# Window attention and a maxout layer in chunks of 256 tokens: h of the later chunks two chunks at a time, and written-out slots

## The chip, the cores and the metric

The kernel runs on one core of a Trainium2 chip. Its time is the device time of one launch in microseconds (us), given as the median of several runs, with the lowest and the highest beside it. One further execution is recorded by the hardware profiler; its span runs from the first to the last instruction.

## The reference

Attention over a sliding window of 128 positions, plus the first four positions of each sequence as "sinks", and behind it a layer that takes the largest of three products:

```python
# q, k, v: [4, 8, 768, 64], float32
scores = scale * np.matmul(q, k.transpose(0, 1, 3, 2))
...
in_window = (rel >= 0) & (rel < int(window))
keep = is_sink | in_window
scores = np.where(keep, scores, -1000000000.0)
...
a = np.exp(scores)
a = a / (np.sum(a, axis=-1, keepdims=True) + 1e-09)
attn_out = np.matmul(a, v)
...
# x: [3072, 512]; w1, w2, w3: [512, 768]; w_out: [768, 512]
h = np.maximum(np.maximum(x @ w1, x @ w2), x @ w3)
return (h @ w_out).astype(np.float32)
```

There are 4 batches of 768 tokens, 8 heads of 64, and 3072 tokens in the second part.

## The kernel before

The tokens are cut into 12 chunks of 256, three for each batch (`CPB`); each partition holds two neighbouring tokens, and heads go in four pairs. A chunk passes these steps, each a function that is called with the chunk's number:

- `load` (L90) brings q, k and v as float32 on SyncE's (SP's) DMA queue, 512 KB each. The raw tiles have two buffers, so the load of chunk c waits until chunk c-2 has been cast. A gate (`pool_gate`, `after`) is a tiny instruction on POOL that holds a load back until POOL, or a weight, has come that far.
- `cast_qk` (L102) and `cast_v` (L108) write bf16 copies, on POOL, ACT or VectorE (DVE), whichever the call names.
- `turn` and `turn2` transpose q and k on TensorE for the first four chunks; from chunk 4 on `turn_dma` (L157, L162) does it with DMA transposes on SP's queue, two issues for k and one for q. The transposed tiles (`kT`, `qT`) and `vb` are rings of four.
- `score` (L278): six matmuls for each head pair into two PSUM banks; `expo` (L290) takes the exponentials on ACT and frees the banks; `mask` (L296) zeroes on VectorE what lies outside the window. `premask` adds a mask on TensorE instead, for some pairs at the start.
- `sink_k`, `sink_score` (L304, L310), `sink_v` (L320): the same for the four sink tokens.
- `av` (L354, and L336 for the sinks): probabilities times v, with a column of ones for the sum; VectorE takes the reciprocal (L359) and writes x (`x_sb`, L362).
- `xpose` (L375) transposes x on TensorE for chunks 0 to 3, `xpose_dma` (L381) by DMA on SP's queue for the others.
- `ffn_h(ci, fp, wi)` (L394): eight matmuls of 256 columns, two blocks of 128 hidden units for one of the three weights, into one PSUM bank. The first weight's bank is copied by ACT (L401), the other two are folded in by VectorE with a maximum (L405). A chunk has nine such groups.
- `ffn_y` (L415): six matmuls of 512 columns for each half of a chunk, then a copy by ACT or VectorE (L417), and `store` (L431) on SP's queue. The last chunk's second half goes in two parts (`ffn_y_part`, L425; `store_half`).

PSUM has eight banks; `bank` hands them out in the order in which `give` returned them while the program was written, so that a step waits for the release of the bank that it was given. `warm` runs matmuls on zeros at the start. TensorE is PE in the views.

The order is set by hand: each engine executes its instructions in the order of the calls, and SP's queue issues its DMAs in that order too. Chunks 0 to 3 are listed call by call. Behind them a loop runs over slots: slot i scores chunk i+1, computes h of chunk i and y of chunk i-1, and loads, casts and transposes chunk i+3, with a fixed order for all slots but the first and the last two.

Of the kernel before, what the change touches and what calls it, by code (L numbers as in the profile page):

```python
# [9 lines left out]
F32 = mybir.dt.float32  # L10
# [6 lines left out]
def kernel(  # L17
# [31 lines left out]
    with tc.manual_schedule():  # L49
# [316 lines left out]
        xTs = {}  # L366

# [39 lines left out]

        ys = {}

        def ffn_y(ci, t, eng=None):  # L410
# [3 lines left out]
            for fb in range(FB):  # L414
                nc.tensor.matmul(yp, lhsT=hs[ci][:, fb, t * 128:(t + 1) * 128], rhs=wo[:, fb],  # L415
# [4 lines left out]
        def ffn_y_part(ci, t, c0, c1, eng):  # L420
# [3 lines left out]
            for fb in range(FB):  # L424
                nc.tensor.matmul(yp, lhsT=hs[ci][:, fb, t * 128:(t + 1) * 128],  # L425
# [33 lines left out]
        load(0, 'q', gate=pool_gate)  # L459
        masks()  # L460
        cast_qk(0, 'q', 1, nc.vector)
        warm(4)
        premask(0, (2,))
        premask(0, (0,))
        warm(9)
        cast_qk(0, 'k', 0, nc.scalar)
        turn(0, 'k', 0, nc.vector)
        load(0, 'v')
        cast_qk(0, 'q', 0, nc.scalar)
        turn(0, 'q', 1, nc.vector)  # L470
        sink_init()
        warm(1)
        cast_qk(0, 'k', 1, nc.gpsimd)
        cast_v(0, 1, 0, nc.vector)
        turn(0, 'k', 1, nc.scalar)
        load(1, 'k')
        turn(0, 'q', 0, nc.scalar)
        cast_v(0, 0, 1, nc.vector)
        score(0, (2,))
        masks_late()  # L480
        premask(0, (1,))
        load_w(0, 512, 768)
        load_w(0, 0, 512)
        cast_v(0, 0, 0, nc.vector)
        load(1, 'q')
        score(0, (0,))
        sink_k(0)
        expo(0, 2)
        load_w(1, 512, 768)
        cast_qk(1, 'k', 0, nc.vector)  # L490
        expo(0, 0)
        premask(0, (3,))
        cast_v(0, 1, 1, nc.vector)
        cast_qk(1, 'q', 0, nc.gpsimd)
        score(0, (1,))
        premask(1, (1,))
        turn2(1, 'k', 0, nc.vector)
        cast_qk(1, 'k', 1, nc.scalar)
        score(0, (3,))
        expo(0, 1)  # L500
        cast_qk(1, 'q', 1, nc.gpsimd)
        load(1, 'v')
        turn2(1, 'k', 1, nc.scalar)
        expo(0, 3)
        av_open(0)
        av(0, 0)
        av(0, 1)
        sink_v(0)
        turn2(1, 'q', 0, nc.vector)
        load_w(1, 0, 512)  # L510
# [385 lines left out]
```

## Time and profile before

| | |
|---|---|
| median of 3 runs | 179.18 us (179.01 to 179.55) |
| the profiled execution | 179.04 us, of it 177.3 us span |
| mean granted TensorE clock | 0.996 of full speed |
| L394, h matmuls of 256 columns | 864, 100.7 us busy |
| L415, y matmuls of 512 columns | 138, 32.4 us busy |
| L290, exponentials on ACT | 96, 46.6 us busy |
| L405, maxima on VectorE | 74, 49.2 us busy |
| data moved | 34.90 MB, 197 GB/s mean |

A duration of a matmul in the groups is longer than its share of the time, because matmuls overlap; where the text needs what one adds, it takes a stretch of the chain of waits and divides by the count. The share of busy time is a mean over the whole program: what a wait costs is read in the stretch in which it stands.

### The profile page before, as it was taken

The page shows a single profiled execution, that of the slowest core. Times are in us where ns is not written, and L with a number is a line of the kernel's source. Part 1 is how long each engine was busy: PE and PEld are TensorE (multiplying, and loading weights), DVE is VectorE, ACT ScalarE, POOL GpSimd, SP SyncE. Part 2 cuts the span into 40 slices and gives each one's busy share as a digit, 9 for nine tenths or more (in the row PEclk, how much of TensorE's full clock was granted, in tenths as well). Part 3 has the DMA queues.
Part 4 walks back from the last instruction along what each step waited for, and adds up shares of the span by engine and source line. Part 5 has one row for each costly group of instructions (what it writes and reads, how often), then busy time and mean ns, then how long its engine had stood idle before and what let it go on. Part 6 is the DMA issues. An engine that isn't in the chain of part 4 may idle for free.

```text
span 177.3 us, 4632 instructions
## 1 busy us (share of the span) xinstructions
PE 170.1 (96%) x1872; PEld 127.1 (72%) x1872; DVE 126.5 (71%) x267; ACT 85.8 (48%) x171; POOL 67.1 (38%) x123
## 2 busy tenths in 40 slices
PE   6899999999998999999999999999999999999991
PEld 2446889856895597697696696796795895796870
DVE  3389738699698578796884984975885875966451
ACT  3498732577924822913724814814616617320210
POOL 6884344146580274544724624417427000000000
PEclk9999999999999999999999999999999999999998
DMA  5999999995999969999999999999999519305203
GB/s 141 290 287 203 224 248 259 216 265 148 290 140 236 94 142 299 129 245 173 251 269 189 210 301 160 213 303 153 198 293 198 150 34 379 125 11 170 120 0 118
DMA packets 69573, 34.90 MB, mean 197 GB/s; under 512 B 26544, under 2 KB 68016, under 8 KB 69552
## 3 DMA queue, kind: packets, MB, share of 16 engines
q1 hardware_dynamic: 64912, 31.33, 81.3%
q0 software_dynamic: 4496, 3.15, 11.6%
q8 instruction: 14, 0.23, 0.5%
q10 hardware_dynamic: 144, 0.13, 0.2%
q14 instruction: 7, 0.06, 0.1%
HBM read 25.17 MB, written 6.29 MB: 177 GB/s over the span
## 4 chain that ended last, share of the span: by engine, by line
PE 87%; DMA 4%; DVE 3%; SPq 2%; POOL 1%; ACT 1%; issue 0%; POOLq 0%
PE h_ps L394 52%; PE y_ps L415 18%; PE o L354 6%; PE st L278 6%; DMA q_raw<-in_q_dram 4%; SPq L90 2%; DVE h_sb L405 1%; PE o L336 1%; PE sk L304 1%; PE pt L118 1%; PE y_ps L425 1%; DVE x_sb L362 1%; POOL q_bf L102 1%; PE xt L375 1%; DVE vb L108 0%
## 5 line engine op out<-in xcount | busy, mean ns | idle before, releaser
L394 PE MATMUL h_ps<-xT,w 128*128 128x256 bf16 x864 | 100.7, 273 | 0.1
L394 PEld LDWEIGHTS <-w 128*128 128x128 bf16 x864 | 82.2, 98 | 10.4 <-issue 0.5
L405 DVE TENSOR_TENSOR h_sb<-h_sb,h_ps 128x512 bf16<-128x512 bf16 (+1 forms) x74 | 49.2, 671 | 21.2 <-PE h_ps L394 19.4
L290 ACT ACTIVATE e_sb<-st 128x512 bf16<-128x512 f32 (+1 forms) x96 | 46.6, 579 | 5.9 <-PE st L278 5.8
L401 ACT CAST h_sb<-h_ps 128x512 bf16<-128x512 f32 x36 | 21.2, 588 | 43.1 <-PE h_ps L394 42.9
L108 POOL CAST vb<-v_raw 64x512 bf16<-64x512 f32 x38 | 28.0, 737 | 15.8 <-DMA v_raw<-in_v_dram 14.5
L296 DVE TENSOR_TENSOR e_sb<-e_sb,msk 128x1024 bf16<-128x1024 bf16 (+1 forms) x42 | 31.6, 786 | 2.5 <-ACT e_sb L290 2.3
L415 PE MATMUL y_ps<-wo,h_sb 128*128 128x512 bf16 x138 | 32.4, 379 | 0.2 <-DVE h_sb L405 0.2
L415 PEld LDWEIGHTS <-h_sb 128*128 128x128 bf16 x138 | 12.6, 98 | 14.8 <-issue 1.6
L362 DVE TENSOR_TENSOR x_sb<-o,rc 128x256 bf16<-128x256 f32 x48 | 20.4, 425 | 1.6
L102 POOL CAST k_bf<-k_raw 128x512 bf16<-128x512 f32 x17 | 10.3, 625 | 28.5 <-DMA k_raw<-in_k_dram 28.5
L102 POOL CAST q_bf<-q_raw 128x512 bf16<-128x512 f32 x21 | 13.3, 658 | 16.4 <-DMA q_raw<-in_q_dram 13.0
L417 DVE COPY y_sb<-y_ps 128x512 f32<-128x512 f32 x13 | 9.0, 691 | 13.7 <-PE y_ps L415 13.7
L354 PE MATMUL o<-vb,e_sb 128*128 128x65 bf16 x352 | 16.5, 193 | 0.0
L354 PEld LDWEIGHTS <-e_sb 128*128 128x128 bf16 x352 | 14.6, 97 | 2.0 <-DVE e_sb L296 0.2
L278 PE MATMUL st<-qT,kT 64*128 64x128 bf16 (+1 forms) x256 | 14.5, 238 | 0.5 <-ACT kT L125 0.5
L278 PEld LDWEIGHTS <-kT 64*128 64x128 bf16 x256 | 8.1, 94 | 7.1 <-issue 4.9
L310 ACT ACTIVATE e_sink<-sk 128x256 bf16<-128x256 f32 x8 | 3.1, 385 | 14.8 <-PE sk L304 14.8
L359 DVE RECIPROCAL rc<-o 128x4 f32<-128x4 f32 x48 | 8.4, 175 | 1.3 <-PE o L354 1.0
L417 ACT COPY y_sb<-y_ps 128x512 f32<-128x512 f32 x10 | 5.9, 586 | 3.3 <-PE y_ps L415 2.7
L102 ACT CAST k_bf<-k_raw 128x512 bf16<-128x512 f32 x5 | 3.1, 626 | 6.5 <-DMA k_raw<-in_k_dram 6.5
L180 PE MATMUL warm<-wz 128*128 128x512 bf16 x14 | 4.5, 462 | 1.2 <-DVE wz L169 1.2
(69 smaller groups left out, 72.7 us busy)
## 6 DMA issues: line engine op xcount, KB each, us to landing
k_raw<-in_k_dram SPq DMA_DIRECT2D x12, 512.0 KB, 5.5
q_raw<-in_q_dram SPq DMA_DIRECT2D x12, 512.0 KB, 7.0
v_raw<-in_v_dram SPq DMA_DIRECT2D x12, 512.0 KB, 8.2
out_dram<-y_sb SPq DMA_DIRECT2D x11, 512.0 KB, 4.0
w<-in_moe_w_dram POOLq DMA_DIRECT2D x5, 256.0 KB, 8.7
w<-in_moe_w_dram POOLq DMA_DIRECT2D x2, 512.0 KB, 9.8
wo<-in_moe_w_out_dram POOLq DMA_DIRECT2D x2, 384.0 KB, 9.8
kT<-k_bf SPq DMA_TRANSPOSE x16, 3.7
```

The costliest lines, as they stand in the source:

```text
L102: f(x[:, 2 * g:2 * g + 2].rearrange("q p i a d -> q p a i d"), y[:, 4 * g:4 * g + 4].rearrange("q (p a) i d -> q p a i d", a=2))
L108: eng.tensor_copy(vb[ci % RING][64 * i:64 * i + 64, n, :, 0:D], raws[ci, "v"][64 * n:64 * n + 64, :, i])
L278: nc.tensor.matmul(st[a][:, s:s + q1 - q0].rearrange("q n (i r) -> q n i r", i=2), lhsT=x[hp, n, p].rearrange("q i r -> q (i r)"), rhs=qc[ ...
L290: nc.scalar.activation(e[:, a, lo:], st[a][:, lo:], AF.Exp, scale=scale)
L296: (eng or nc.vector).tensor_mul(e[:, :, lo:], e[:, :, lo:], msk0 if lo else msk)
L354: nc.tensor.matmul(o[:, t, a], lhsT=e[:, a, s], rhs=vb[cv % RING][:, n, 2 * p + a], start=first, stop=True, skip_group_check=True)
L362: nc.vector.tensor_mul(xs[ci][:, :, p], o[:, :, :, 0:D], rc.unsqueeze(3).to_broadcast([128, 2, 2, D]))
L394: nc.tensor.matmul(hp[:, f].rearrange("q (i t r) -> q i t r", i=2, t=2), lhsT=w_sb[wi][:, ds, c0:c0 + 128], rhs=xTs[ci][:, :, ds].rearrang ...
L401: nc.scalar.copy(dst, hp)
L405: nc.vector.tensor_max(dst[:, x], dst[:, x], hp[:, x])
L415: nc.tensor.matmul(yp, lhsT=hs[ci][:, fb, t * 128:(t + 1) * 128], rhs=wo[:, fb], start=(fb == 0), stop=(fb == FB - 1))
L417: (nc.scalar.copy if eng is None else eng.tensor_copy)(ys[ci][:, t], yp)
```

## The change

**The pairs.** From chunk 6 on (`PAIR`), `xpose_dma` writes the transposed x of chunks 6/7, 8/9 and 10/11 into one shared tile, and `ffn_h2` computes h of both chunks with matmuls of 512 columns: four matmuls for one block of 128 hidden units, one bank, one copy or maximum of 512 elements. Eighteen such groups take the place of the eighteen groups of two chunks. `hcols` picks a chunk's columns of the shared h for `ffn_y`. The h matmuls go from 864 of 256 columns to 432 of 256 and 216 of 512.

**The slots.** The loop is gone. Slots are written out, each in an order of its own; those from chunk 6 on treat two chunks, with both chunks' scores, exponentials and av side by side. The lists of chunks 0 to 3 are in a new order too: `warm` runs 12 and 6 matmuls in place of 4, 9 and 1, other loads stand behind gates, and the four `av` of chunk 3 stand together. Casts of q and k go from 38 on POOL, 6 on ACT and 4 on VectorE to 16, 23 and 9; casts of v from 38 on POOL and 10 on VectorE to 37 and 11. `store(0)` is called twice, so that there are 12 whole stores in place of 11; `store(4)` comes near the end.

**On SP's queue**, the loads and transposes of chunks 10 and 11 (`kT_71` and `qT_75` are chunk 10's, `kT_72` and `qT_76` chunk 11's). Before, from the load of chunk 10 to the transposes of chunk 11:

```order
L90 DMA k_raw<-in_k_dram 128x8x128
L90 DMA q_raw<-in_q_dram 128x8x128
L90 DMA v_raw<-in_v_dram 128x8x128
L381 DMA_TRANSPOSE xT<-x_sb 128x8x128
L162 DMA_TRANSPOSE kT_71<-k_bf 128x8x64 x2
L157 DMA_TRANSPOSE qT_75<-q_bf 128x8x128
L431 DMA out_dram<-y_sb 128x1024
L90 DMA k_raw<-in_k_dram 128x8x128
L90 DMA q_raw<-in_q_dram 128x8x128
L90 DMA v_raw<-in_v_dram 128x8x128
L381 DMA_TRANSPOSE xT<-x_sb 128x8x128
L162 DMA_TRANSPOSE kT_72<-k_bf 128x8x64 x2
```

And now, from the same load on:

```order
L90 DMA k_raw<-in_k_dram 128x8x128 x2
L90 DMA v_raw<-in_v_dram 128x8x128
L90 DMA q_raw<-in_q_dram 128x8x128 x2
L90 DMA v_raw<-in_v_dram 128x8x128
L466 DMA out_dram<-y_sb 128x1024
L162 DMA_TRANSPOSE kT_71<-k_bf 128x8x64 x2
L162 DMA_TRANSPOSE kT_72<-k_bf 128x8x64 x2
L157 DMA_TRANSPOSE qT_75<-q_bf 128x8x128
L466 DMA out_dram<-y_sb 128x1024
L157 DMA_TRANSPOSE qT_76<-q_bf 128x8x128
L384 DMA_TRANSPOSE xT<-x_sb 128x8x128 x2
```

The six loads of the pair now stand together ahead of its transposes, and the transposes of x (here chunks 8 and 9) behind them. The row ahead of the loads is the transposed q of chunk 9; one pair earlier, for chunks 8 and 9, the loads stand together too, with stores among them, behind the transposed x of chunk 5.

**On ACT**, around the scores of chunks 8 and 9. Before, from the sink's exponential of chunk 8 to the exponentials of chunk 9 (those with 384 columns, since chunk 9 is the first of its batch):

```order
L310 ACTIVATE e_sink<-sk 128x256
L290 ACTIVATE e_sb<-st 128x512 x6
L417 COPY y_sb<-y_ps 128x512
L290 ACTIVATE e_sb<-st 128x512 x2
L401 CAST h_sb<-h_ps 128x512 x3
L290 ACTIVATE e_sb<-st 128x384 x6
```

And now the same exponentials:

```order
L290 ACTIVATE e_sb<-st 128x512 x2
L310 ACTIVATE e_sink<-sk 128x256
L290 ACTIVATE e_sb<-st 128x512 x6
L429 CAST h_sb<-h_ps 128x512 x2
L290 ACTIVATE e_sb<-st 128x384 x6
L429 CAST h_sb<-h_ps 128x512
L102 CAST k_bf<-k_raw 128x2x2x2x64
```

The copy of y has gone to VectorE, two copies of h stand between the two chunks' exponentials, and a cast of k stands behind them.

**On VectorE**, chunk 3: from the last mask of its scores to the h of chunk 2 behind its x. Before:

```order
L296 TENSOR_TENSOR e_sb<-e_sb,msk_101 128x2x384 x3
L405 TENSOR_TENSOR h_sb<-h_sb,h_ps 128x512
L359 RECIPROCAL rc<-o 128x4
L362 TENSOR_TENSOR x_sb<-o,rc 128x2x128
L405 TENSOR_TENSOR h_sb<-h_sb,h_ps 128x512
L359 RECIPROCAL rc<-o 128x4
L362 TENSOR_TENSOR x_sb<-o,rc 128x2x128
L108 CAST vb_77<-v_raw 64x8x64
L359 RECIPROCAL rc<-o 128x4
L362 TENSOR_TENSOR x_sb<-o,rc 128x2x128
```

And now, from the maximum behind the last mask on:

```order
L413 TENSOR_TENSOR h_sb<-h_sb,h_ps 128x512
L359 RECIPROCAL rc<-o 128x4
L362 TENSOR_TENSOR x_sb<-o,rc 128x2x128
L359 RECIPROCAL rc<-o 128x4
L362 TENSOR_TENSOR x_sb<-o,rc 128x2x128
L359 RECIPROCAL rc<-o 128x4
L362 TENSOR_TENSOR x_sb<-o,rc 128x2x128
L359 RECIPROCAL rc<-o 128x4
L362 TENSOR_TENSOR x_sb<-o,rc 128x2x128
L413 TENSOR_TENSOR h_sb<-h_sb,h_ps 128x512 x4
```

The four pairs of reciprocal and product of chunk 3 stand together; a cast of v and a maximum that stood between them have moved.

The diff, cut to the functions, the end of chunk 3's list, the order that the loop gave to most slots, and the slot of chunks 8 and 9:

```diff
         xTs = {}
+        PAIR = 6
         def xpose(ci, t, eng=None):
             eng = eng or nc.scalar
@@ -377,6 +378,13 @@
             give(pt)
         def xpose_dma(ci, eng=None):
+            if ci >= PAIR:
+                if ci % 2 == 0:
+                    xTs[ci] = work.tile([128, 2, 2, DS, 128], BF16, tag="xT2", bufs=2, name="xT")
+                (eng or nc.sync).dma_start_transpose(
+                    out=xTs[ci - ci % 2][:, ci % 2].rearrange("q t s r -> q (t s) r"),
+                    in_=xs[ci].rearrange("q t p a d -> q (t p a d)"))
+                return
             xTs[ci] = work.tile([128, 2, DS, 128], BF16, tag="xT", bufs=3, name="xT")
             (eng or nc.sync).dma_start_transpose(
                 out=xTs[ci].rearrange("q t s r -> q (t s) r"),
@@ -405,6 +413,33 @@
                     nc.vector.tensor_max(dst[:, x], dst[:, x], hp[:, x])
             give(hp)
+        def ffn_h2(ci, fb, wi, cuts=1):
+            if ci not in hs:
+                hs[ci] = work.tile([128, FB, 512], BF16, tag="h2", bufs=2, name="h_sb")
+            hp = bank([128, 512], F32, "h_ps")
+            for ds in range(DS):
+                nc.tensor.matmul(
+                    hp.rearrange("q (i c r) -> q i c r", i=2, c=4),
+                    lhsT=w_sb[wi][:, ds, fb * 128:fb * 128 + 128],
+                    rhs=xTs[ci][:, :, :, ds].rearrange("q c t (i r) -> q i (c t) r", i=2),
+                    start=(ds == 0), stop=(ds == DS - 1))
+            dst = hs[ci][:, fb]
+            if wi == 0:
+                nc.scalar.copy(dst, hp)
+            else:
+                for f in range(cuts):
+                    x = slice(512 * f // cuts, 512 * (f + 1) // cuts)
+                    nc.vector.tensor_max(dst[:, x], dst[:, x], hp[:, x])
+            give(hp)
+        def hcols(ci, fb, i):
+            if ci < PAIR:
+                return hs[ci][:, fb, i * 128:(i + 1) * 128]
+            o = i * 256 + ci % 2 * 128
+            return hs[ci - ci % 2][:, fb, o:o + 128]
...
...
-                nc.tensor.matmul(yp, lhsT=hs[ci][:, fb, t * 128:(t + 1) * 128], rhs=wo[:, fb],
+                nc.tensor.matmul(yp, lhsT=hcols(ci, fb, t), rhs=wo[:, fb],
-                nc.tensor.matmul(yp, lhsT=hs[ci][:, fb, t * 128:(t + 1) * 128],
+                nc.tensor.matmul(yp, lhsT=hcols(ci, fb, t),
...
+        ffn_h(2, 2, 0)
+        cast_v(4, 0, 1, nc.gpsimd)
+        cast_qk(4, 'k', 1, nc.vector)
+        cast_v(3, 1, 1, nc.vector)
+        load(5, 'q')
         mask(3, 0)
-        cast_v(3, 0, 0, nc.gpsimd)
-        score(3, (2,))
-        cast_v(3, 0, 1, nc.gpsimd)
-        cast_qk(4, 'q', 1, nc.gpsimd)
-        cast_qk(4, 'k', 1, nc.gpsimd)
-        cast_qk(4, 'k', 0, nc.vector)
+        mask(3, 2)
+        cast_qk(4, 'q', 0, nc.scalar)
+        ffn_h(2, 2, 1)
         ffn_h(2, 1, 0)
-        expo(3, 2)
-        expo(3, 3)
-        ffn_h(2, 1, 1)
-        cast_qk(4, 'q', 0, nc.gpsimd)
-        mask(3, 1)
-        mask(3, 3)
-        mask(3, 2)
-        ffn_h(2, 2, 0)
         ffn_h(2, 0, 0)
         av_open(3)
+        mask(3, 3)
+        ffn_h(2, 1, 1)
         turn_dma(4, 'k')
-        ffn_h(2, 2, 1)
+        av(3, 0)
         turn_dma(4, 'q')
+        av(3, 2)
+        load(5, 'v', gate=after(0))
+        av(3, 1)
+        load(5, 'k')
+        cast_v(4, 1, 0, nc.gpsimd)
+        cast_v(4, 0, 0, nc.gpsimd)
         av(3, 3)
-        load(5, 'v', gate=after(0))
         ffn_h(2, 0, 2)
-        av(3, 0)
-        cast_v(4, 0, 1, nc.vector)
-        cast_v(4, 1, 0, nc.gpsimd)
-        load(5, 'q')
-        av(3, 2)
-        cast_v(4, 1, 1, nc.gpsimd)
-        av(3, 1)
         ffn_h(2, 0, 1)
         ffn_h(2, 1, 2)
+        xpose(3, 1, nc.scalar)
+        xpose(3, 0, nc.scalar)
         ffn_h(2, 2, 2)
-        xpose(3, 0, nc.vector)
-        cast_v(4, 0, 0, nc.gpsimd)
-        xpose(3, 1, nc.scalar)
...
-            elif n % CPB:
-                load(i + 3)
-                sink_score(n)
-                score(n, (0,))
-                expo(n, 0)
-                score(n, (3,))
-                score(n, (1,))
-                expo(n, 1)
-                expo(n, 3)
-                ffn_y(m, 0, nc.vector)
-                mask(n, 0)
-                ffn_y(m, 1)
-                score(n, (2,))
-                mask(n, 3)
-                av_open(n)
-                mask(n, 1)
-                expo(n, 2)
-                av(n, 0)
-                mask(n, 2)
-                ffn_h(i, 1, 0)
-                ffn_h(i, 0, 0)
-                av(n, 1)
-                ffn_h(i, 1, 2)
-                ffn_h(i, 0, 1)
-                cast_qk(i + 3, 'k', 0, nc.gpsimd)
-                cast_qk(i + 3, 'k', 1, nc.gpsimd)
-                cast_qk(i + 3, 'q', 0, nc.gpsimd)
-                cast_qk(i + 3, 'q', 1, nc.gpsimd)
-                cast_v(i + 3, 0, 0, nc.gpsimd)
-                cast_v(i + 3, 0, 1, nc.gpsimd)
-                cast_v(i + 3, 1, 0, nc.gpsimd)
-                cast_v(i + 3, 1, 1, nc.gpsimd)
-                av(n, 2)
-                av(n, 3)
-                ffn_h(i, 1, 1)
-                ffn_h(i, 2, 0)
-                ffn_h(i, 0, 2)
-                ffn_h(i, 2, 1)
-                xpose_dma(n)
-                turn_dma(i + 3, 'k')
-                turn_dma(i + 3, 'q')
-                store(i - 4)
-                ffn_h(i, 2, 2, 1 if i + 2 < NCH else 2)
...
+        ffn_y(5, 0, nc.vector)
+        load(10, 'k')
+        score(8, (0,))
+        score(8, (1,))
+        expo(8, 0)
+        load(11, 'k', gate=pool_gate)
+        sink_score(8)
+        load(11, 'v', gate=pool_gate)
+        ffn_y(5, 1, nc.vector)
+        expo(8, 1)
+        score(8, (3,))
+        load(11, 'q')
+        expo(8, 3)
+        load(10, 'q', gate=pool_gate)
+        score(8, (2,))
+        mask(8, 1)
+        expo(8, 2)
+        load(10, 'v', gate=pool_gate)
+        store(3)
+        ffn_h2(6, 3, 0)
+        ffn_h2(6, 0, 0)
+        score(9, (1,))
+        score(9, (0,))
+        score(9, (2,))
+        expo(9, 1)
+        mask(8, 2)
+        mask(8, 3)
+        expo(9, 0)
+        ffn_h2(6, 3, 2)
+        expo(9, 2)
+        mask(8, 0)
+        ffn_h2(6, 2, 0)
+        cast_qk(10, 'k', 1, nc.gpsimd)
+        cast_qk(10, 'k', 0, nc.scalar)
+        mask(9, 1)
+        ffn_h2(6, 1, 0)
+        cast_qk(11, 'k', 0, nc.vector)
+        ffn_h2(6, 1, 1)
+        cast_qk(11, 'q', 1, nc.gpsimd)
+        cast_qk(11, 'k', 1, nc.vector)
+        mask(9, 2)
+        score(9, (3,))
+        cast_qk(11, 'q', 0, nc.gpsimd)
+        cast_v(10, 0, 1, nc.gpsimd)
+        av_open(8)
+        cast_qk(10, 'q', 1, nc.gpsimd)
+        turn_dma(10, 'k')
+        turn_dma(11, 'k')
+        av(8, 2)
+        av(8, 0)
+        sink_k(3)
+        av(8, 3)
+        expo(9, 3)
+        ffn_h2(6, 5, 0)
+        ffn_h2(6, 1, 2)
+        mask(9, 0)
+        ffn_h2(6, 4, 0)
+        ffn_h2(6, 0, 2)
+        mask(9, 3)
+        ffn_h2(6, 2, 1)
+        av_open(9)
+        ffn_h2(6, 5, 1)
+        av(9, 1)
+        ffn_h2(6, 2, 2)
+        cast_qk(10, 'q', 0, nc.scalar)
+        turn_dma(10, 'q')
+        av(8, 1)
+        ffn_h2(6, 5, 2)
+        av(9, 2)
+        ffn_h2(6, 3, 1)
+        ffn_h2(6, 0, 1)
+        av(9, 0)
+        ffn_h2(6, 4, 2)
+        av(9, 3)
+        store(5)
+        ffn_h2(6, 4, 1)
+        cast_v(11, 0, 0, nc.gpsimd)
+        turn_dma(11, 'q')
+        xpose_dma(8)
...
```

More of the change, by code (lines that the diff above doesn't have):

```diff
@@ L574 @@
+        ffn_h(1, 2, 2)
+        ffn_h(0, 2, 2)
+        cast_v(2, 1, 0, nc.gpsimd)
         load(4, 'q')
[L575 removed]
+        mask(2, 2)
+        cast_qk(3, 'k', 1, nc.gpsimd)
         score(2, (1,))
[L577 to L588 removed]
```

639 lines of the change are left out of this document (383 added, 256 removed).

## The prediction

> **What bounds the kernel now.** I read the page first: busy shares, slices, chain.
>
> ```profile
> span 177.3 us, 4632 instructions
> PE 170.1 (96%) x1872; PEld 127.1 (72%) x1872; DVE 126.5 (71%) x267; ACT 85.8 (48%) x171; POOL 67.1 (38%) x123
> PE   6899999999998999999999999999999999999991
> DMA  5999999995999969999999999999999519305203
> PE 87%; DMA 4%; DVE 3%; SPq 2%; POOL 1%; ACT 1%; issue 0%; POOLq 0%
> ```
>
> TensorE stands at 9 in every slice but the first two, the 13th (53 to 58 us) and the last, and carries 87% of the chain. The DMA row is what else to keep in mind: it stands at 9 up to slice 31 (some 142 us) and is low after. Then the chain in order of time, to see where it leaves PE and at what pace PE works:
>
> ```profile
> 20.99 0.45 PE xt L375 x8
> ...
> 51.58 0.04 issue
> 51.62 0.68 DVE h_sb L405
> ...
> 56.62 1.46 PE y_ps L415 x6
> ...
> 121.53 0.18 PE sv L320 x8
> 121.71 0.60 PE st L278 x12
> ...
> 147.42 0.55 PE st L278 x12
> ...
> 160.48 2.59 PE y_ps L415 x12
> 163.07 7.86 PE h_ps L394 x72
> ```
>
> From 58 us to 173.5 the chain never leaves PE: nothing but PE's own instructions sets the time there. The one long absence is 51.58 to 56.62, and PE's timeline shows it as two short waits for VectorE:
>
> ```profile
> 51.58 2.78 PE L394 MATMUL h_ps<-xT,w 128*128 128x256 bf16 x24
> 54.20 0.22 PE L375 MATMUL xt<-ident,x_sb 128*128 128x128 bf16 x1
> 54.84 0.56 PE L375 MATMUL xt<-ident,x_sb 128*128 128x128 bf16 x7 [0.41 <-DVE x_sb L362]
> 55.33 0.25 PE L320 MATMUL sv<-vb,sel 128*32 128x65 bf16 x8
> 55.51 0.89 PE L278 MATMUL st<-qT,kT 64*128 64x128 bf16 x12
> 56.62 0.59 PE L415 MATMUL y_ps<-wo,h_sb 128*128 128x512 bf16 x2 [0.22 <-DVE h_sb L405]
> ```
>
> At PE's own pace this stretch is 24 h matmuls (24 x 0.1092 = 2.62, the 0.1092 being 7.86 / 72), eight transposes (0.45), the eight sink sums (0.18) and twelve score matmuls (0.60): 3.85 us. It took 56.62 - 51.58 = 5.04. So **1.2 us** are lost there, and it is the only sizeable loss after the start.
>
> **The 512 columns.** A 256-column h matmul takes 7.86 / 72 = 109.2 ns. The y matmuls already have 512 columns, a new stationary operand each and the same start-to-start rhythm: 2.59 / 12 = 215.8 ns. Chunks 6 to 11 have 432 h matmuls before and 216 after, so PE saves 216 x (2 x 109.2 - 215.8) = 216 x 2.6 = **0.56 us**. That is all: the columns streamed stay the same. ACT's copies and VectorE's maxima keep their number and their 512 elements, one after four matmuls in place of one after eight, so they cost the same. The h matmul of after reads four runs of 64 columns for each half where it read two; the 256-column form already reads runs of 64 and streams at full pace, so I price this at nothing (bounds: 0, and the 0.56 us gone).
> By the Trainium skill ("TensorE: Matmul & The Clock Gate", Back-to-back issue gap) a stream of weight loads and matmuls sustains about 131 ns for each matmul of 512 columns, which would make this step, as an estimate from that page, 216 x (218 - 131) ns = 19 us. The row of twelve y matmuls, 215.8 ns each with a weight load apiece, says otherwise, and the row decides.
>
> **Groups of score matmuls.** Runs of two chunks now stand side by side. Counted over the program, PE's entries into these narrower matmuls (scores, sinks, sink sums) from full-width ones go from 28 to 30, so nothing is won by that: priced 0, bounds plus or minus 0.3 us.
>
> **The start.** Loads, casts and the first scores are reordered, and there are four more warming matmuls. What decides when PE is fed is further on:
>
> ```profile
> 18.82 1.05 PE L394 MATMUL h_ps<-xT,w 128*128 128x256 bf16 x8
> 18.83 0.18 POOL L441 CAST k_raw<-w 1x1 f32<-1x1 bf16 x1 [3.37 <-DMA w<-in_moe_w_dram]
> ```
>
> POOL's gate and PE's second h group start together when the second piece of the first weight lands. In both programs six raw loads and the first weight piece stand ahead of it, and in both PE has by then to do the first h group and 24 av matmuls of chunk 1. I see after reaching that point some 0.4 us earlier and waiting there: 0, bounds plus or minus 0.4.
>
> **Chunks 2 to 5.** After puts the four av of chunk 3 together ahead of three h groups (24 x 0.1092 = 2.62 us), keeps casts of v off VectorE between them, and moves y of chunk 2 from behind the first scores of chunk 4 to 61 us. The two VectorE waits above lose their cause: minus **1.2 us** (bounds: none of it, all of it). Late next there is the last x_sb of chunk 3, which I find on time by about 0.3 us.
>
> **What must now be early.** Two chunks' attention runs ahead of their common h, so attention comes earlier against PE's work. After the first score pair of chunk 11, PE still has 36 h groups (36 x 4 x 0.2158 = 31.1), ten y halves (10 x 1.295 = 13.0) and about 3.2 us of scores and av. So that pair is due near 173 - 47.3 = 125.5 us; before it came at 147.42. The transposed q of chunk 11 was issued as follows:
>
> ```profile
> 135.46 1.26 SPq L157 DMA_TRANSPOSE qT<-q_bf  x1
> qT<-q_bf SPq DMA_TRANSPOSE x8, 3.2
> 4.92 0.62 ACT L102 CAST k_bf<-k_raw 128x512 bf16<-128x512 f32 x1 [2.67 <-DMA k_raw<-in_k_dram]
> 6.72 0.51 DVE L102 CAST q_bf<-q_raw 128x512 bf16<-128x512 f32 x1 [2.90 <-DMA q_raw<-in_q_dram]
> 8.53 0.97 DVE L108 CAST vb<-v_raw 64x512 bf16<-64x512 f32 x2 [0.39 <-DMA v_raw<-in_v_dram]
> 105.17 1.17 POOL L102 CAST k_bf<-k_raw 128x512 bf16<-128x512 f32 x2 [4.77 <-DMA k_raw<-in_k_dram]
> 107.80 1.18 POOL L102 CAST q_bf<-q_raw 128x512 bf16<-128x512 f32 x2 [1.47 <-DMA q_raw<-in_q_dram]
> 109.73 0.61 POOL L108 CAST vb<-v_raw 64x512 bf16<-64x512 f32 x1 [0.75 <-DMA v_raw<-in_v_dram]
> 99.43 0.44 SPq L90 DMA_DIRECT2D k_raw<-in_k_dram  x1
> ```
>
> It landed near 135.46 + 3.2 = 138.7, so it has to be 13 us earlier. Casts wait for loads: 1.8 us apart (4.92, 6.72, 8.53) when only loads run, 2.3 (109.73 - 105.17 over two) among other traffic, the first 5.7 after its issue (105.17 - 99.43).
> For chunks 8 and 9, SP may issue the first load only behind the transposed x of chunk 5, ready near 79, so near 80.2. Then come 5.7 us, five loads and two stores at 1.8 (12.6): 98.5. Behind them the k transposes and q of chunk 8 need 1.5 to 3.9 us (three issues of 1.26): 100 to 102. The first score of chunk 8 is due at 99.4. Short by 0.6 to 3: I take **plus 0.7**, near the pure pace, since six loads now follow one another with only stores between; bounds 0 and, at 2.3 for each of the seven, 0.7 + 7 x 0.5 = 4.2.
> For chunks 10 and 11 the same sum runs from 101.5 (behind x of 7 and q of 9): 5.7 + 5 x 1.8 + a store 1.8 = 118, then two sets of transposes and a store, 5 to 8 us: 123 to 126 for a need at 125.5 plus the shift from chunk 8. Priced 0.
>
> **ACT at chunks 8 and 9.** ACT takes casts from POOL (23 of k and q, 6 before), and here its exponentials pile up:
>
> ```profile
> 95.77 3.04 ACT L290 ACTIVATE e_sb<-st 128x512 bf16<-128x512 f32 x6
> 47.16 1.65 ACT L290 ACTIVATE e_sb<-st 128x384 bf16<-128x384 f32 x4
> 48.66 1.23 ACT L401 CAST h_sb<-h_ps 128x512 bf16<-128x512 f32 x2
> ```
>
> From the first score of chunk 8 PE works 5.2 us (seven score pairs 1.9, a y half 1.3, two h groups 1.7, a sink 0.2) until its third h group needs the bank that ACT's first h copy frees. Up to it ACT has eight exponentials (8 x 0.507), the sink's (0.4) and the copy (0.6): 5.1 us, begun 0.4 after the scores. **Plus 0.4**; bounds 0 and 1.9 (ACT's whole 8.8 us, with six exponentials of 0.41 and two copies more, against 6.9 of PE). VectorE's extra casts lie beside PE work; where its cast of k of chunk 11 is late, chunk 8's masks queue behind it, which is in the bounds.
>
> **Sum.** 179.04 (this execution: 177.3 and 1.7 around it) - 0.56 - 1.2 + 0.7 + 0.4 = 178.4. The median of the runs shown, 179.18, is 0.14 above that execution, so I forecast **178.5**. A second store of chunk 0 and the late store of chunk 4 lie on a queue that is nearly empty after 142 us; what PE does last is the same.
>
> **Rivals.**
> Nothing new waits (0.18): the loads keep 1.8 and ACT keeps up. 179.18 - 1.76 = 177.4. For it: PE's unbroken chain from 58 on; against it: the sums for chunk 8.
> The queue becomes the bound (0.25): PE waits for q of chunk 8 and then for x of 6 and 7, and k of chunk 11 blocks VectorE. At half the extra pace (0.25 x 7 = 1.8) plus a miss of 1.5 at chunks 10 and 11: 177.4 + 0.7 + 1.8 + 1.5 = 181.4 with little more for ACT. It turns the result slower once these waits together pass 1.8 us, that is when q of chunk 8 lands after about 101. For it: the DMA row at 9; against: 13.16 us slots with three loads, three transposes and a store left room.
> The gain is eaten in small waits (0.17): ACT's upper bound, or the VectorE waits of chunk 3 kept: 179.2 to 179.4. That 512 columns don't reach 215.8 (then the 0.56 is missing) ends here too.
> My own case has 0.40.
>
> **How the numbers follow.** Two runs' medians can be told apart from about 0.3%, 0.54 us: faster is under 178.64, slower over 179.72. Of my case 0.32 lies under 178.64 and 0.08 within; with 0.18 of the first rival faster is 0.50. The small waits give 0.12 within and 0.05 beyond; 0.02 of the queue's case is within: same 0.22, slower 0.28. The range runs from the first rival less 0.3 for start and groups, 177.1, into the queue's case to 181.4; beyond it lies about 0.2.
>
> **What would show it.** h matmuls of 512 columns at 216 ns; no VectorE wait near 54 to 57; PE's waits at the first score of chunk 8 (about 99 to 101) and at h of 6 and 7 behind it, released by DMA or ACT; the first score pair of chunk 11 near 125. It would be wrong if PE waits for DMA before chunk 8, if the start moves by over 0.4 us, or if h takes over 220 ns.

## The result

| | before | changed |
|---|---|---|
| median (runs) | 179.09 us (4; 178.78 to 179.55) | 186.44 us (4; 186.30 to 188.59) |
| ratio, 95% interval | | 1.0436 (1.0357 to 1.0515) |
| profiled execution, span | 179.04, 177.3 us | 186.30, 184.5 us |

The forecast was 178.5 us and a range up to 181.4. The kernel became 4.4% slower.

### The profile page after: what moved, and what is told of

The parts are those of the page before. It is cut to its first block, busy times and chain, and to the rows that moved or that the text cites. A ratio compares the mean times of both kernels' runs of the same rounds, so it can differ in the third digit from the quotient of the medians.

```text
span 184.5 us, 4227 instructions
## 1 busy us (share of the span) xinstructions
PE 172.0 (93%) x1660; PEld 106.7 (58%) x1660; DVE 125.7 (68%) x274; ACT 93.0 (50%) x186; POOL 49.4 (27%) x110
## 3 DMA queue, kind: packets, MB, share of 16 engines
q0 software_dynamic: 4496, 3.15, 11.1%
## 4 chain that ended last, share of the span: by engine, by line
PE 63%; DMA 20%; DVE 6%; ACT 5%; issue 2%; SPq 1%; POOL 1%; POOLq 0%
PE h_ps L422 26%; PE h_ps L402 13%; PE y_ps L450 12%; DMA w<-in_moe_w_dram 8%; DMA q_raw<-in_q_dram 5%; DMA qT<-q_bf 5%; PE st L278 4%; PE o L354 4%; ACT e_sb L290 4%; DMA xT<-x_sb 2%; DVE h_sb L413 2%; DVE e_sb L296 1%; PE pt L118 1%; DVE x_sb L362 1%; PE y_ps L460 1%
## 5 line engine op out<-in xcount | busy, mean ns | idle before, releaser
L422 PE MATMUL h_ps<-xT,w 128*128 128x512 bf16 x216 | 51.0, 388 | 3.0 <-DMA xT<-x_sb 3.0
L402 PE MATMUL h_ps<-xT,w 128*128 128x256 bf16 x432 | 51.8, 273 | 1.0 <-ACT e_sb L290 0.7
L402 PEld LDWEIGHTS <-w 128*128 128x128 bf16 x432 | 40.5, 98 | 7.3 <-DMA xT<-x_sb 0.9
L422 PEld LDWEIGHTS <-w 128*128 128x128 bf16 x216 | 20.6, 99 | 27.1 <-issue 5.2
L433 DVE TENSOR_TENSOR h_sb<-h_sb,h_ps 128x512 bf16<-128x512 bf16 (+1 forms) x37 | 24.5, 669 | 14.8 <-PE h_ps L422 13.7
L108 POOL CAST vb<-v_raw 64x512 bf16<-64x512 f32 x37 | 23.8, 644 | 36.0 <-PE h_ps L402 16.5
L413 DVE TENSOR_TENSOR h_sb<-h_sb,h_ps 128x512 bf16<-128x512 bf16 x36 | 24.2, 682 | 10.1 <-PE h_ps L402 9.5
L296 DVE TENSOR_TENSOR e_sb<-e_sb,msk 128x1024 bf16<-128x1024 bf16 (+1 forms) x42 | 28.2, 698 | 4.0 <-ACT e_sb L290 3.9
L452 DVE COPY y_sb<-y_ps 128x512 f32<-128x512 f32 x15 | 10.4, 690 | 11.2 <-PE y_ps L450 11.2
L102 POOL CAST k_bf<-k_raw 128x512 bf16<-128x512 f32 x7 | 4.8, 682 | 21.0 <-DMA k_raw<-in_k_dram 19.8
L102 ACT CAST q_bf<-q_raw 128x512 bf16<-128x512 f32 x13 | 8.1, 628 | 3.2 <-issue 1.9
```

What stands on the lines that cost most here:

```text
L108: eng.tensor_copy(vb[ci % RING][64 * i:64 * i + 64, n, :, 0:D], raws[ci, "v"][64 * n:64 * n + 64, :, i])
L296: (eng or nc.vector).tensor_mul(e[:, :, lo:], e[:, :, lo:], msk0 if lo else msk)
L402: nc.tensor.matmul(hp[:, f].rearrange("q (i t r) -> q i t r", i=2, t=2), lhsT=w_sb[wi][:, ds, c0:c0 + 128], rhs=xTs[ci][:, :, ds].rearrang ...
L413: nc.vector.tensor_max(dst[:, x], dst[:, x], hp[:, x])
L422: nc.tensor.matmul(hp.rearrange("q (i c r) -> q i c r", i=2, c=4), lhsT=w_sb[wi][:, ds, fb * 128:fb * 128 + 128], rhs=xTs[ci][:, :, :, ds] ...
L433: nc.vector.tensor_max(dst[:, x], dst[:, x], hp[:, x])
```

## The profile after

The page of the changed kernel: busy time, the slices of PE, of its granted clock and of the DMA engines, and the chain by engine.

```profile
span 184.5 us, 4227 instructions
PE 172.0 (93%) x1660; PEld 106.7 (58%) x1660; DVE 125.7 (68%) x274; ACT 93.0 (50%) x186; POOL 49.4 (27%) x110
PE   7999999999999998889999659999999999999991
PEclk9999999999999999999999978999999999999998
DMA  4999999999789988999999999999800550000085
PE 63%; DMA 20%; DVE 6%; ACT 5%; issue 2%; SPq 1%; POOL 1%; POOLq 0%
```

PE's share of the chain fell from 87% to 63%, the transfers' rose from 4% to 20%. PE has holes from slice 16 on and a deep one in slices 23 and 24, and right behind it the granted clock drops. PE's timeline shows each hole with what ended it (start, duration, instructions, idle before them):

```profile
72.62 1.05 PE L402 MATMUL h_ps<-xT,w 128*128 128x256 bf16 x8 [0.67 <-ACT e_sb L290]
...
76.97 0.41 PE L354 MATMUL o<-vb,e_sb 128*128 128x65 bf16 x8 [0.74 <-DVE e_sb L296]
...
83.48 0.84 PE L278 MATMUL st<-qT,kT 64*128 64x128 bf16 x18 [1.20 <-DMA qT<-q_bf]
...
102.61 0.61 PE L278 MATMUL st<-qT,kT 64*128 64x128 bf16 x12 [0.80 <-DMA qT<-q_bf]
...
108.40 3.52 PE L422 MATMUL h_ps<-xT,w 128*128 128x512 bf16 x8 [3.00 <-DMA xT<-x_sb]
```

In order: the first h of chunk 4, av of chunk 5, the scores of chunk 7, those of chunk 8, and the first h of chunks 6 and 7. The idle times add up to 6.4 us. In the last row eight matmuls take 3.52 us, 440 ns each; further on in the same chain of waits they take 216:

```profile
98.35 4.22 DMA qT<-q_bf
...
103.75 4.51 DMA xT<-x_sb
...
163.94 3.45 PE h_ps L422 x16
```

The table by stretches gives the clock that was granted to the eight, 0.52 of full speed (its columns: the stretch, then busy time of PE, weight loads, VectorE, ACT and POOL, then granted clock, DMA share, GB/s):

```profile
108.40:111.85 3.45, 3.45 (x8) 0.99 (x9) 0.27 (x1) 0.59 (x1) 0.00 (x0) 0.52 0.87 226
```

A group of eight such matmuls lasts 1.90 us at full clock (run fill12, below). So 1.6 us (3.52 - 1.90) go to a halved clock behind the longest wait. With 6.4 that is 8.0, and 186.3 - 8.0 = 178.3: outside these places PE works within 1 us of the pace that the prediction's first rival named, 177.4. The timeline of SP shows where the transfers stand, before and after. Before (the load of chunk 8, x of chunk 6, then the transposes of chunk 8; the last row is PE at the scores of chunk 8):

```profile
86.68 0.44 SPq L90 DMA_DIRECT2D k_raw<-in_k_dram  x1
...
92.48 2.09 SPq L381 DMA_TRANSPOSE xT<-x_sb  x1
94.67 2.54 SPq L162 DMA_TRANSPOSE kT<-k_bf  x2
97.32 1.25 SPq L157 DMA_TRANSPOSE qT<-q_bf  x1
...
108.51 0.84 PE L278 MATMUL st<-qT,kT 64*128 64x128 bf16 x18
```

After (q of 8 behind x of 5; q of chunk 8 transposed; then k of 9 and x of 6 and 7):

```profile
80.36 1.90 SPq L389 DMA_TRANSPOSE xT<-x_sb  x1
82.36 0.54 SPq L90 DMA_DIRECT2D q_raw<-in_q_dram  x1
...
95.01 3.25 SPq L162 DMA_TRANSPOSE kT<-k_bf  x2
98.35 1.33 SPq L157 DMA_TRANSPOSE qT<-q_bf  x1
99.78 2.53 SPq L162 DMA_TRANSPOSE kT<-k_bf  x2
102.40 3.87 SPq L384 DMA_TRANSPOSE xT<-x_sb  x2
```

PE needs chunk 8 some 9 us earlier than before (99.4, by the prediction's count, against 108.5), but its transposed q is issued 1.0 us later (98.35 against 97.32). Before, with some 3.2 us from issue to landing, it lay ready at about 100.5, 8 us ahead of its use; now it lands at 102.6, 3 us after the time at which it was to be used. Nothing has become much slower on the queue: the order asks for the same transfers earlier, and they don't come earlier.

**The theory:** the loads, stores and transposes nearly fill the DMA engines, so that a transfer comes earlier by little more than what is taken from ahead of it, and the pairs ask for it earlier. **Rivals:** the 512 columns themselves cost; the order in which SP issues costs, at bytes that would fit; ACT and VectorE can't serve two chunks side by side.

## The experiments

Times are medians; each ratio is to before, measured on the same chip beside it (178.9 to 179.5 us).

### The columns, the clock

**h256**: the same pairs and order, each 512-column matmul split.

```diff
-            for ds in range(DS):
-                nc.tensor.matmul(hp..., rhs=xTs[ci]..., ...)
+            for i in range(2):
+                for ds in range(DS):
+                    nc.tensor.matmul(hp...[:, i], ..., rhs=xTs[ci]...[:, i], ...)
```

> The changed kernel with each 512-column h matmul split into two of 256 columns into the same bank; order, copies and waits unchanged. If the waits for transfers make the loss, the split costs what two narrower matmuls cost in the trace, 216 x (2 x 109.2 - 215.8) ns = 0.56 us: 186.8 to 187.1. If the form of 512 columns over two chunks itself makes the loss, most of the 7 us come back: 180 to 182.

186.41 us, 1.0410 (1.0368 to 1.0452): no difference from the changed kernel. The form of 512 columns costs nothing, and the 0.56 us that it saves don't show either while PE waits for transfers behind it.

**fill12**: dummy matmuls into the bank in which PE waits.

```diff
+            for _ in range(fill):
+                nc.tensor.matmul(hp, lhsT=wz[:, 0:128], rhs=wz, start=True, stop=True)
...
-        ffn_h2(6, 3, 0)
+        ffn_h2(6, 3, 0, fill=12)
```

> The changed kernel with twelve dummy matmuls of zeros, 512 columns, written into the bank of the first h of chunks 6 and 7 ahead of it (2.6 us of PE work inside its wait of 3 us). If the eight h matmuls of 427 ns behind that wait come from the idle time of PE, they run at 216 and the time falls by 8 x 0.211 = 1.7 us to 184.7. If they are slow for their operands, or the half clock has another cause, 186.4.

184.79 us, 1.0314 (1.0288 to 1.0340): 1.65 less than the changed kernel, with twelve more matmuls. PE's timeline at the same place:

```profile
104.98 2.76 PE L422 MATMUL h_ps<-wz 128*128 128x512 bf16 x12
107.96 1.90 PE L424 MATMUL h_ps<-xT,w 128*128 128x512 bf16 x8 [0.22 <-DMA xT<-x_sb]
```

The eight real matmuls now take 1.90 us where they took 3.52. The half clock comes from PE's idle time, and 2.8 us of PE work in that hole were free. The run shows one thing more: the dummies write into the bank from 104.98 on, with no idle time behind the scores, so the bank was free by then, and what the first h waits for is x alone.

### Fewer bytes

**stores_late**, **stores_end**: stores taken from ahead of the transposes.

```diff
 # stores_late
-        store(1)
...
-        store(0)
...
         xpose_dma(7)
+        store(1)
 # stores_end: y with 11 buffers, no earlier store, and
         xpose_dma(11)
+        store(0)
...
+        store(7)
```

> The changed kernel without the second store of chunk 0, and with the store of chunk 1 moved behind the transposes of x of chunks 6 and 7: two transfers of 512 KB (1.3 to 1.8 us each) fewer ahead of q of chunk 8 and of those transposes. If transfers ahead in the queue set when they land, they land some 2.6 to 3.6 us earlier: the wait at the scores of chunk 8 (0.96) goes, that at h of 6 and 7 shrinks from 3.2 to under 0.8 and the half clock behind it (1.7) goes: 181 to 182. If the wait is for x itself or for the order of issues, 186.

> The changed kernel with eleven buffers for y, all stores of chunks 0 to 7 behind the transposed x of chunk 11, and one store of chunk 0: three transfers fewer ahead of the transposes of x of 6 and 7, one of them ahead of q of chunk 7, two more ahead of chunk 10 and 11. If transfers ahead on the queue set the waits: that for q of chunk 7 (1.4) goes, as do q of chunk 8 (1.0) and the half clock (1.7), and the wait at h of 6 and 7 falls under 0.8: 179.5 to 181. If the queue's order of loads alone decides, as late as the run without two of these stores: 183 to 184.

183.93 us, 1.0274 (1.0212 to 1.0335), and 181.57, 1.0153 (1.0123 to 1.0183). In the first, PE still idled 1.5 us ahead of the first h of chunks 6 and 7, where it had been 3.0, and 0.7 and 1.0 us ahead of the scores of chunks 9 and 10, where it had not waited before; in the second the longest wait fell to 1.1 and the mean granted clock rose from 0.988 to 1.000. Both went the way of the theory and both fell short of what was expected, the first by 2 to 3 us, the second by 0.6. The new waits at chunks 9 and 10 suggest why: once PE comes earlier, it meets the next transposes earlier too.

**no_loads**, **no_traffic**: loads of chunks 7 to 11 left out (their casts read older raw tiles), and in the second the stores as in stores_end too.

```diff
+            if ci >= 7:
+                for w in what:
+                    raws[ci, w] = raws[ci - 2, w]
+                return
```

> The changed kernel without the loads of chunks 7 to 11: their casts read the raw tiles of two chunks earlier, all casts, transposes, scores and stores are still done. If late loads on SP's queue make the loss, its waits at chunks 5, 7, 8 and at h of 6 and 7 go, with the half clock: 177.4 to 178.5, the price of the case in which nothing new waits, plus the wait of 0.9 at the first h of chunk 4. If the transposes on that queue, or ACT and VectorE, are too slow for two chunks side by side, over 181.

> The changed kernel without loads of chunks 7 to 11 and with all stores behind the last transposes: from 58 to 130 us SP's queue has only transposes left. If the 1.7 us that the run without loads still stood above before come from the stores, 179.3. If they come from the order of transposes and from VectorE (waits of 0.7, 0.9 and 0.7 at h of chunk 4, of 5 and of 6 and 7), about what the run without loads gave: 180.3 to 181.

180.98 us, 1.0106 (1.0076 to 1.0136), and 179.64, 1.0026 (1.0009 to 1.0042). The first lies between the two expectations (178.3 to 179.4, and over 181); the second is within 0.4 us of the case in which the stores make the rest. So 6.8 of the 7.4 us hang on loads and stores. What is left of waits in no_traffic is for transposes of x, with no load or store of the later chunks beside them:

```profile
72.12 1.05 PE L406 MATMUL h_ps<-xT,w 128*128 128x256 bf16 x8 [0.74 <-DMA xT<-x_sb]
...
103.33 1.02 PE L426 MATMUL h_ps<-xT,w 128*128 128x512 bf16 x4 [0.93 <-DMA xT<-x_sb]
```

The first stands behind six transposes of chunks 5 and 6, for which SP takes 9.6 us; the second lands 4 us behind the x that it transposes, and the slot leaves PE no more than about 3.

**half_loads**: every issue in its place, four of eight heads (half the bytes, so half the packets).

```diff
+                if ci >= 7:
+                    nc.sync.dma_start(
+                        out=dst[:, 0:4],
+                        in_=src[b, 0:4, t0:t0 + 256]...)
+                    continue
```

> The changed kernel with the loads of chunks 7 to 11 cut to four of eight heads: as many issues in the same order on SP, half the bytes; the casts read these four heads twice. If it is the bytes that the queue has to move, 15 loads at half of 1.8 us bring nearly what leaving them out brought (186.4 to 181.0): 181 to 182.5. If it is the number and the order of issues on SP, 185 to 186.4.

179.85 us, 1.0062 (1.0042 to 1.0082): even more than expected, and at least as good as leaving the loads out (why it is 1.1 us better than that is open). With the same issues in the same order the loss is nearly gone, so the number and order of SP's issues don't make it alone; what they move does. The table by stretches shows where. The changed kernel:

```profile
91.00:104.00 13.00, 12.20 (x146) 7.81 (x145) 10.46 (x24) 5.76 (x12) 5.80 (x10) 1.00 1.21 233
104.00:117.00 13.00, 10.01 (x80) 4.23 (x79) 5.32 (x10) 8.91 (x21) 1.27 (x6) 0.87 1.12 222
```

half_loads, in the same stretches:

```profile
91.00:104.00 13.00, 12.33 (x142) 7.48 (x143) 10.71 (x23) 7.46 (x17) 7.17 (x14) 1.00 0.77 147
104.00:117.00 13.00, 13.00 (x108) 6.31 (x106) 10.54 (x21) 8.20 (x18) 6.63 (x11) 1.00 1.09 222
```

The DMA share falls from 1.21 to 0.77 in the stretch in which the transposes of chunks 8 and 9 and of x of 6 and 7 are issued, and PE is busy throughout the next one, 13.00 us against 10.01.

The kernel before:

```profile
78.00:91.00 13.00, 13.00 (x147) 9.95 (x144) 10.19 (x21) 5.52 (x12) 5.87 (x10) 1.00 1.13 229
91.00:104.00 13.00, 13.00 (x153) 9.85 (x151) 9.97 (x20) 6.68 (x13) 5.59 (x8) 1.00 1.12 235
104.00:117.00 13.00, 13.00 (x152) 9.83 (x151) 9.65 (x20) 6.68 (x13) 5.16 (x8) 1.00 1.11 224
```

The share counts overlapping packets, so it can pass 1. In the kernel before it stands at 1.1 in these three stretches, each about one slot of 13.16 us long, while PE is busy all of it; the stretches beside them have 1.05 (from 65 us) and 0.90 (from 130). The highest that such a stretch of the changed kernel reaches is 1.24. So the transfers left the engines little room before, too. They were only early enough not to be seen. (How much room a share of 1.1 leaves, no run measures.)

### The same bytes in another order

**loads_ahead**, **k8_ahead**, **k7_first**, **v9_late**: four orders on SP's queue. What stands ahead of what, in the first three:

```diff
 # loads_ahead: chunk 7 ahead of the transposes of 6, chunk 8 ahead of those of 7
-        turn_dma(6, 'k')
+        load(7, 'k', gate=pool_gate)
+        load(7, 'q')
...
         xpose_dma(4)
+        turn_dma(6, 'k')
+        turn_dma(6, 'q')
...
+        load(8, 'k', gate=pool_gate)
+        load(8, 'q', gate=pool_gate)
         turn_dma(7, 'k')
 # k8_ahead: load(7, 'q') behind xpose_dma(4); load(8, 'k') without its gate; load(8, 'q') behind xpose_dma(5)
 # k7_first: as k8_ahead on stores_end, load(8, 'k') behind turn_dma(7, 'q')
 # v9_late: as k7_first, load(9, 'v') and its casts behind turn_dma(9, 'q'), load(11, 'v') some calls later
```

> The changed kernel with the same transfers in another order on SP's queue: loads of k and q of chunk 7 ahead of the transposes of chunk 6, x of chunk 4 ahead of these too, loads of k and q of chunk 8 ahead of the transposes of chunk 7. If the late issue of these loads makes the loss, the waits at chunk 5 (0.9 and 0.9), 7 (1.4), 8 (1.0), at h of 6 and 7 (3.2) and the half clock (1.7) go for the most part: 177.5 to 179.5. If the transfers together are too much for the queue whatever their order, 183 to 186.

> The changed kernel with the same transfers, SP's queue in an order nearer to before's: k of chunk 7 ahead of the transposed x of chunk 4, its q and then the transposes of chunk 6 behind it, k of chunk 8 (without a gate on POOL) ahead of the transposes of chunk 7, q of chunk 8 right behind x of chunk 5. If the order in which these stand makes the loss, the waits of 0.9 at chunk 5, 1.4 at chunk 7 and 1.0 at chunk 8 go and that at h of 6 and 7 falls to about 0.5 without half clock: 178 to 180. If the sum of the transfers is too much for the queue in any order, 184 to 187.

> The kernel with all stores at the end (181.6), and on SP's queue k of chunk 7 ahead of the transposed x of chunk 4, its q and the transposes of chunk 6 behind that, k of chunk 8 only behind the transposes of chunk 7 and its q behind x of 5. If it is the bytes ahead of each transpose that count, nothing stands ahead of chunk 7's any longer: the waits of 0.5, 1.1 and 1.0 at chunks 4, 5 and 7 go and h of 6 and 7 comes 2 us earlier: 179 to 180. If the queue holds the same work either way, 181 to 182.

> As k7_first, with the load of v of chunk 9 and its casts moved behind the transposes of chunks 8, 9 and of x of 6 and 7: 512 KB fewer ahead of these. If the bytes ahead count, x of 7 lands 1.3 to 1.8 us earlier than in k7_first and no wait at h of 6 and 7 is over 0.4: 178.2 to 179. If it was not the bytes, as k7_first.

188.90 us, 1.0552 (1.0510 to 1.0594); 187.47, 1.0457 (1.0410 to 1.0503); 183.16, 1.0211 (1.0188 to 1.0235), slower than stores_end on which it was built; and v9_late 1.0302 (1.0233 to 1.0371), its runs scattered from 183.74 to 188.03, so no better than k7_first. All four lie above even the worse of their two expectations. None won; each moved the wait. In loads_ahead the fault is partly mine: the gate of k of 8 stood on POOL behind a cast that waited, so SP stood still from 75.6 to 80.1. k8_ahead has no such gate, and shows what order does at the same bytes:

```profile
76.78 0.42 SPq L90 DMA_DIRECT2D k_raw<-in_k_dram  x1
77.38 4.26 SPq L162 DMA_TRANSPOSE kT<-k_bf  x2
81.73 2.83 SPq L157 DMA_TRANSPOSE qT<-q_bf  x1
```

The transposes of chunk 7 behind that load take 4.26 and 2.83 us to issue, where the changed kernel had 2.52 and 1.26, and PE waits 5.07 us for chunk 7. So order moves the waits at the same bytes; the whole time of k8_ahead can't be told from the changed kernel's, that of k7_first is 0.6% above stores_end. These four runs don't show that no order fits; they show that four guesses at one didn't.

**k7_on_pool**: a wait upstream of the queue taken away.

```diff
-        cast_qk(7, 'k', 1, nc.vector)
+        cast_qk(7, 'k', 1, nc.gpsimd)
```

> The changed kernel with VectorE's cast of k of chunk 7, which waits for its load and holds two masks of chunk 5 back (PE's wait of 0.9 at 76 us), moved to POOL. If SP's queue alone sets when PE goes on at chunks 7 to 9, that wait goes and the next ones grow by as much: 186.4 to 187 (POOL then does both halves of k, up to 0.6 later). If PE's waits simply add up, 186.4 - 0.9 = 185.5.

187.78 us, 1.0452 (1.0429 to 1.0475), 0.8 us above the range expected. The wait at 76 us is gone and the next one has grown past it:

```profile
85.44 1.46 PE L278 MATMUL st<-qT,kT 64*128 64x128 bf16 x18 [3.99 <-DMA qT<-q_bf]
...
110.92 1.89 PE L422 MATMUL h_ps<-xT,w 128*128 128x512 bf16 x8 [2.97 <-DMA xT<-x_sb]
```

PE's waits at chunks 5 to 7 don't add up: the transfers set when PE goes on, and here, with both halves of k cast on POOL, the transposed q of chunk 7 is issued 1.6 us later still.

**loads_on_pool**, **loads_on_pool_stores_end**: the loads of chunks 7 to 11 from POOL's queue.

```diff
-                    nc.sync.dma_start(
+                    (nc.gpsimd if ci >= 7 else nc.sync).dma_start(
```

> The changed kernel with the loads of chunks 7 to 11 issued by POOL, on its own queue, in the same order among POOL's work; transposes and stores stay on SP's. If the loss comes from one queue in which a transpose waits behind loads, transposes land about 3 us after their issue, and the waits at chunks 7, 8 and at h of 6 and 7 fall under 1 us together, without half clock: 180 to 182. If the transfers share the DMA engines and these are full, 185 to 187.

> As loads_on_pool, with all stores of chunks 0 to 7 behind the last transposes and eleven buffers for y. If bytes decide on whatever queue, 181.6 as with the stores at the end alone, within 1 us. If the one queue decides, 178 to 179.5, near the run that has neither loads nor stores in the way (179.6).

210.02 us, 1.1736 (1.1663 to 1.1810); the second 202.0 to 209.5, too scattered for a ratio. Both expectations of each are missed by far. The transposes, alone with the stores on SP's queue now, land later than ever; the chain of waits of loads_on_pool has

```profile
69.26 10.30 DMA xT<-x_sb
...
87.26 17.69 DMA xT<-x_sb
```

A queue of their own for the loads did not help. The Trainium skill ("DMA: Bandwidth & Descriptors", Issuing engines are not separate DMA queues) says as much: DMAs of all issuing engines end up on the same 16 DMA engines and interleave, and a second issuer saves only the time to issue. This run agrees so far as the second issuer gained nothing; that the transposes of x fare worse than in one queue (17.7 us from issue to landing, where the changed kernel has 4.6 at most) goes beyond it, and why is left open.

### The lists alone

**lists_only**: the new lists of chunks 0 to 3 ahead of before's loop. **lists_v6_late**: the same, with v of chunk 6 loaded behind x of chunk 4.

```diff
 # lists_v6_late against lists_only, slot 3
-                load(i + 3)
+                load(i + 3, 'kq')
...
                 xpose_dma(n)
+                load(i + 3, 'v')
+                cast_v(i + 3, 0, 0, nc.gpsimd)
...
```

> The changed kernel's lists of chunks 0 to 3 with the loop of before behind them: no pairs, no 512 columns, SP's queue in before's order from chunk 5 on. If the lists took VectorE's two waits away (1.2 us) and the start is neutral, 179.2 - 1.2 = 178.0, and PE's waits of over 0.5 us behind the start are gone. If the lists cost something that the losses at chunks 5 to 9 hid, or make chunk 4 and 5 late on the queue, 179.2 or more.

> As lists_only (179.6), with the load of v of chunk 6 and its casts moved from ahead of the transposed x of chunk 4 to behind it: 512 KB fewer ahead of that transpose, for which PE waits 0.56 us at the first h of chunk 4. If bytes ahead on the queue are what a transpose waits for, it lands some 1.8 us earlier, the wait goes, and 179.0 to 179.2 is left, 0.1 to 0.3 under before measured beside it. If not, 179.6.

lists_only gave 179.62 us, 1.0023 (1.0006 to 1.0040), the second of its two expectations. VectorE's two waits are gone, and two others have come:

```profile
29.02 1.92 PE L394 MATMUL h_ps<-xT,w 128*128 128x256 bf16 x16 [0.43 <-DMA w<-in_moe_w_dram]
...
68.99 0.84 PE L278 MATMUL st<-qT,kT 64*128 64x128 bf16 x18
...
73.82 1.91 PE L394 MATMUL h_ps<-xT,w 128*128 128x256 bf16 x16 [0.40 <-DMA xT<-x_sb]
```

The scores of chunk 5 begin at 68.99; in the kernel before they began at 69.66. The lists are 0.7 us ahead there, and the transposed x of chunk 4 eats most of it. lists_v6_late moved 512 KB from ahead of that transpose and gave **178.58 us**, 0.9978 (0.9956 to 1.0000), against 179.30 beside it, 0.4 us better than expected: the wait is gone.

```profile
73.24 0.42 PE L354 MATMUL o<-vb,e_sb 128*128 128x65 bf16 x8
73.49 1.91 PE L394 MATMUL h_ps<-xT,w 128*128 128x256 bf16 x16
```

This version beats the changed kernel by 4% and before by 0.2%, the latter at the edge of its interval.

## Why the prediction was wrong

- **The bound.** PE was named, rightly. The DMA row at 9 was quoted as something to keep in mind, and not priced: the table by stretches would have shown 1.1 in the slots from 78 to 117 us. (The row was read as 9 throughout; slices 10 and 15 have 5 and 6.) A resource that is nearly full beside the bound has little room to deliver anything sooner.
- **What must now be early** is the step that failed: "plus 0.7". It began at chunk 8. The queue was late from chunk 4 on: x of 4 behind six transposes (it landed together with the end of ACT's last exponential, which the row at 72.62 names), k of 7 (which held a mask of 5 back), q of 7; 2.6 us of PE's waits lie ahead of chunk 8. The prediction had named a wait for DMA before chunk 8 as a sign that it is wrong. For chunk 8 the sum was nearly right, q landing at 98.35 + 4.22 = 102.6 against "100 to 102", but partly by luck: k's transposes were issued at 95.0, ahead of the 98.5 of the sum, and q landed 7.6 us behind that in place of 1.5 to 3.9. PE, late by then, waited only 0.8 us for it. But x of 6 and 7, behind k of 9 on the same queue, landed at 103.75 + 4.51 = 108.3 (VectorE had written it by 101.3), and my own case had no term for it. That wait of 3.0 us appears in a rival with a chance of 0.25, inside a lump of 1.8 us for the whole queue.
- **The half clock**, 1.6 us, was in no case, and fill12 shows it to be real. Without it the result would be that of fill12, 184.8, still outside the range.
- **The rival "the queue becomes the bound"** was the right mechanism, with its point of decision (q of chunk 8 after about 101) passed as written. Its price, 181.4, had the waits with half the extra pace, nothing ahead of chunk 8 and no halved clock; 186.4 was measured.
- **Chunks 2 to 5, minus 1.2:** right in the mechanism. The waits went; some 0.5 came back at the start, where the weight lands at 29 us (the bounds for the start were 0.4), and 0.7 was left until the queue took it. lists_v6_late keeps 0.7 by the medians, 0.4 by the ratio.
- **The 512 columns:** 3.45 us for 16 matmuls, 215.6 ns each, as priced; in the whole kernel the gain is not seen (h256).
- **ACT at chunks 8 and 9, plus 0.4:** no run shows this wait. In the changed kernel PE waits for transfers just ahead. With half the loads a row names ACT:

```profile
100.13 1.82 SPq L394 DMA_TRANSPOSE xT<-x_sb  x1
...
103.42 0.81 PE L432 MATMUL h_ps<-xT,w 128*128 128x512 bf16 x3 [0.56 <-ACT e_sb L300]
```

But x of 7, issued at 100.13, takes 3.15 us to land, at 103.28, just as an exponential ends; PE goes on 0.14 us behind it, as in the changed kernel (108.26 and 108.40); in stores_late, stores_end and k8_ahead, whose rows at this place name ACT too, x of 7 lands 0.13 us ahead of PE. And in fill12 the bank was free 2.7 us behind the first score of chunk 8, which would be 102.8 here. So this wait is for x as well, and with half the loads the rival that ACT can't serve two chunks side by side finds no support.

- **Chunks 10 and 11, priced 0:** no wait for them in the changed kernel, but that doesn't bear the price out: PE is 7 us late by then (first score of chunk 11 at about 132.8 against 125.5, or 125.7 by the terms of its sum), and q of 11 is issued only at 125.76. Where PE came earlier, it waited for chunk 10, 0.45 us in fill12 and 0.95 in stores_late:

```profile
126.88 0.84 PE L278 MATMUL st<-qT,kT 64*128 64x128 bf16 x18 [0.95 <-DMA qT<-q_bf]
```

## What to carry to other kernels

Before moving work earlier, read the DMA share of each stage beside the busy time of the bound: if it stands near the highest that the kernel reaches anywhere, a transfer that has to come sooner must displace another one. Here fewer bytes ahead of it helped each time that loads or stores were cut, four new orders of the pairs' transfers did not, and one moved load in the kernel of lists did. Price a late transfer from the first place at which the new order needs one, not from the place that looks critical, and follow it to the last one in the queue (here x of 6 and 7). An early gain is kept only if what waits next is also moved: the same 1.2 us was worth nothing in lists_only and 0.4 to 0.7 us after one load had changed its place.

## What the hardware showed that was not expected

PE idle for 3.0 us cost another 1.6 us of halved clock (440 ns for each of eight matmuls), where idle times of 1.2 and 0.8 us cost none. The length alone doesn't decide. In h256 an idle time of 2.86 us halved the clock (granted 0.55), and in k7_on_pool one of 2.97 us, at the same place of the program, left it whole (granted 1.00):

```profile
108.20:111.60 3.40, 3.40 (x18) 2.30 (x20) 0.40 (x1) 0.58 (x1) 0.00 (x0) 0.55 0.85 215
110.90:112.40 1.50, 1.48 (x7) 0.70 (x8) 0.32 (x1) 0.42 (x1) 0.00 (x0) 1.00 0.61 114
```

The Trainium skill ("TensorE: Matmul & The Clock Gate", Part 1) has the clock fall to half after an idle window of about 3.4 us that runs freely. These traces differ in the length, since gaps of 2.86 and 3.00 us were enough; that one of 2.97 was not fits a window that runs freely, in which it counts where the gap falls. Dummy matmuls in the gap kept the clock whole (fill12, mean granted clock 1.000 against 0.988). And a second DMA queue made the first one's transposes of x slower, from 4.6 to 17.7 us in the worst case, at bytes unchanged.
